# Taking whole turns off in PSUM: the phases of the kernel generation move from VectorE to TensorE

## The chip, the cores and the metric

One core of a Trainium2 chip runs the program. The time is the device time of one execution in microseconds; the kernel before was timed three times and its median is given. A profile of one further execution shows what each engine did.

## The reference

Four layers are applied to a sequence of 2048 rows of 640 channels: a state-space convolution, attention, the same convolution and the same attention again, each on the layer-normed input and added to it. The part that matters here is the kernel `K` of the convolution, which both convolution layers use:

```python
dt = jnp.exp(log_dt)[:, None]
A = A_re + 1j * A_im
logdA = dt * A
dB = dt * Bc
P = jnp.exp(logdA[:, :, None] * l[None, None, :])
K = jnp.einsum("dn,dnl,dn->dl", Cc, P, dB).real
...
y = irfft2(rfft2(u padded) * rfft2(K padded))[..., :L] + u * Dskip
```

For each of 640 channels and 2048 positions, `K` is a sum over 128 states of a complex exponential. Its size is the exponential of a real number that grows with the position, and its angle is a phase that grows with it too, many whole turns in all.

## The kernel before, in words

The program first generates `K` (`kgen`), then transforms it, and then runs the layers. The generation splits the position in a coarse and a fine part, so that the exponential is a product of two factors, and sums over the states with matmuls. `kg_tables` computes, per channel and state, the numbers from which all sizes and angles follow, splits each in three bf16 parts and sends them through DRAM into three tables: `tb` (48 rows), `ta` and `tm` (96 rows). A matmul of a table's 48 or 96 rows with the constants in `kg` (0, 1, 2, ... in blocks) then makes 512 columns of angles or sizes at once.

The loop in `_kgen` has 20 units of 32 channels, `u` from 0 to 19, and works on several at once. In iteration `u`, for unit `u`, `u + 1`, `u - 1` and so on:

- `sizes(u, k)`, k = 0, 1, 2: two matmuls each of 512 columns into the PSUM tile `pe` (L404, two buffers), and `exps(u, k)`, an exponential of it on ScalarE (L412, L414).
- `phase_first(u + 1, h)`, h = 0, 1: two matmuls of 512 columns into the PSUM tile `ph` (L371, one buffer), from `tb` (48 rows) for h = 0 and from `ta` (96 rows) for h = 1. The result is an angle in turns.
- `phase(u + 1, h)`: VectorE rounds it to whole turns by adding and subtracting `MAGIC`, 1.5 x 2^23 (L191, into the tile `r`), and subtracts the whole turns (L381, into `f`, four buffers).
- `trig(u, h)`: ScalarE takes the absolute value of `f` (L394), the sine of `f` (L395) and the cosine by way of the absolute value (L396).
- `products(u - 1, k)`: six VectorE operations of 1024 columns that multiply sizes by sines and cosines (L422 to L431).
- `sums(u - 2, ds)`: eight groups of 16 small matmuls (L441) that sum over the states into the PSUM tile `pk`.
- `store(u - 3)`: ScalarE copies `pk` out (L450), and every fourth unit goes to DRAM.

In eight iterations, and after the loop's end, `stats` adds two statistics operations and their merge on VectorE. The order of the instructions on TensorE, ScalarE and VectorE is the order in which the loop writes them (`manual_schedule`), with even and odd iterations written differently so that ScalarE's exponentials and sines need one change of its table per iteration. After the last `sizes` the tables' memory is freed (`early.close()`) and the weights of the first transform are loaded into it.

Of the kernel before, what the change touches and what calls it, by code (L numbers as in the profile page):

```python
# [11 lines left out]
F32 = mybir.dt.float32  # L12
F32R = mybir.dt.float32r
BF16 = mybir.dt.bfloat16
I32 = mybir.dt.int32
AF = mybir.ActivationFunctionType
ALU = mybir.AluOpType
# [4 lines left out]
P = 128  # L22
# [5 lines left out]
MAGIC = 1.5 * 2.0**23  # L28
TWO_PI = 2.0 * math.pi
# [25 lines left out]
def host_constants():  # L55
    i = np.arange(64)
    jh = np.arange(2)
    base = (32 * i[None, :] + 16 * jh[:, None]).reshape(P)
    t = np.arange(8)
    j = np.arange(2)  # L60
    l = base[:, None, None] + t[None, :, None] + 8 * j[None, None, :]
    k1 = np.arange(256)
    ang = (l[..., None] * (4 * k1 + 1)) % 8192
    th = 2.0 * np.pi * ang / 8192.0
    cs = np.stack([np.cos(th), -np.sin(th)], axis=-2)
    cs = cs.reshape(P, 8, 2, 2, 2, P)
    wf = np.ascontiguousarray(cs).astype(np.float32)
    wi = np.ascontiguousarray(cs.transpose(5, 1, 2, 3, 4, 0) / 2048.0).astype(np.float32)

    col = np.arange(32)  # L70
    r1 = np.zeros((96, 16, 32), np.float32)
    r2 = np.zeros((96, 16, 32), np.float32)
    r3 = np.zeros((96, 16, 64), np.float32)
    r4 = np.zeros((96, 16, 32), np.float32)
    for d in range(16):
        for part in range(3):
            row = 16 * part + d
            r1[row, d] = col + 1
            r2[row, d] = col
            r2[48 + row, d] = 1  # L80
            r3[row, d] = 32 * np.arange(64)
            r4[row, d] = col
            r4[48 + row, d] = 1
    kg = np.concatenate([r.reshape(96, -1) for r in (r1, r2, r3, r4)], axis=1)

    ob = np.zeros((P, 6, 64), np.float32)
    for r in range(D):
        ob[r % P, r // P, r // 20] = 1
    ob[32:52, 5, 32] = 1

    row = np.zeros((66, L), np.float32)
    row[0:64:2] = 1
    row[64:] = -1
    return {
        "c_ob": ob.reshape(P, -1),
        "c_row": row,
        "c_wf": wf.reshape(P, -1),
        "c_wi": wi.reshape(P, -1),
        "c_kg": kg.astype(ml_dtypes.bfloat16),
        "c_id": np.eye(P, dtype=np.float32),  # L100
    }
# [55 lines left out]
class Net:  # L157
# [152 lines left out]
    def _kgen(self, ctx):  # L310
        tc, nc, ins = self.tc, self.nc, self.ins
# [5 lines left out]
        ta = sp.tile([96, 8, 5, P], BF16, name="ta")  # L317
        tb = sp.tile([48, 8, 5, P], BF16, name="tb")
        tm = sp.tile([96, 8, 5, P], BF16, name="tm")
        kg = sp.tile([96, 2560], BF16, name="kg")  # L320

        with tc.tile_pool(name="kgq", bufs=1) as pp:
            SH = [P, 5, NST]
# [23 lines left out]

        units = [(q, r, q * 256 + 16 * r, 128, 128) for q in range(2) for r in range(8)]
        units += [(2, r, 512 + 16 * r, 64, 64) for r in range(4)]
        C1, S1, C2, S2, M1, M2, E1R, F, PH, PE_, PK, KST = ({} for _ in range(12))  # L350
        KST[0, 0] = bp.tile([P, 64, 32], F32, tag="kst", bufs=2, name="kst00")

        def big(tag, u, x, bufs=2):
# [8 lines left out]
        def grp(table, u, par, rows):  # L362
            d = units[u][2] + par * units[u][3]
            return table[0:rows, d % 128 // 16, d // 128]

        def phase_first(u, h):

            pp = PH[u, h] = kp.tile([P, 1024], F32, tag="ph", bufs=1, name=f"ph{u}{h}")
            src, col, rows = ((tb, 0, 48), (ta, 512, 96))[h]
            for par in range(2):  # L370
                nc.tensor.matmul(pp[:, 512 * par : 512 * par + 512], grp(src, u, par, rows),  # L371
                                 kg[0:rows, col : col + 512], start=True, stop=True)

        def phase(u, h):
            if (u, h) not in PH:
                phase_first(u, h)
            pp = PH.pop((u, h))
            r = bp.tile([P, 1024], BF16, tag="r", bufs=2, name=f"r{u}{h}")
            self.magic_round(r, pp)
            F[u, h] = bp.tile([P, 1024], F32, tag="f", bufs=4, name=f"f{u}{h}")  # L380
            nc.vector.tensor_tensor(F[u, h], pp, r, ALU.subtract)  # L381

        def trig(u, h):
            if h == 0:
                C1[u], S1[u] = big("c1", u, 33), big("s1", u, 33)
                nc.gpsimd.memset(C1[u][:, :, :, 0:1], 1.0)
                nc.gpsimd.memset(S1[u][:, :, :, 0:1], 0.0)
                s, c = swap(S1[u])[:, :, :, 1:33], swap(C1[u])[:, :, :, 1:33]
            else:
                C2[u], S2[u] = big("c2", u, 32, 3), big("s2", u, 32, 3)  # L390
                s, c = swap(S2[u]), swap(C2[u])
            f = F.pop((u, h))
            fa = bp.tile([P, 1024], F32, tag="fa", bufs=1, name=f"fa{u}{h}")
            nc.scalar.activation(fa, f, AF.Abs)  # L394
            nc.scalar.activation(s, f.rearrange("p (a d s) -> p a d s", a=2, d=16), AF.Sin, scale=TWO_PI)  # L395
            nc.scalar.activation(c, fa.rearrange("p (a d s) -> p a d s", a=2, d=16), AF.Sin,  # L396
                                 scale=-TWO_PI, bias=self.halfpi)

# [17 lines left out]
        def products(u, k):  # L416

            tt = nc.vector.tensor_tensor
            if k == 0:
                E1R[u] = big("e1r", u, 64, 2)  # L420
                er, m1, c1 = (fl(a[u]) for a in (E1R, M1, C1))
                tt(er[:, :, 32:64], m1[:, :, 32:64], c1[:, :, 0:32], ALU.mult)  # L422
                tt(er[:, :, 0:32], m1[:, :, 0:32], c1[:, :, 32:0:-1], ALU.mult)
            elif k == 1:
                m1, s1 = (fl(a.pop(u)) for a in (dict(M1), S1))
                nc.vector.scalar_tensor_tensor(m1[:, :, 32:64], m1[:, :, 32:64], -1.0, s1[:, :, 0:32],
                                               op0=ALU.mult, op1=ALU.mult)
                tt(m1[:, :, 0:32], m1[:, :, 0:32], s1[:, :, 32:0:-1], ALU.mult)
            else:
                tt(C2[u], C2[u], M2[u], ALU.mult)  # L430
                tt(S2[u], S2[u], M2[u], ALU.mult)  # L431
# [34 lines left out]
        with tc.manual_schedule(engines=engines):  # L466
            for h in range(2):
                phase(0, h)
            for u in range(n + 3):
                now, nxt, prod, tot = u < n, u + 1 < n, 0 < u <= n, 2 <= u < n + 2  # L470
                odd = u % 2 == 1
                if u >= 3:
                    store(u - 3)
                if now and not odd:
                    trig(u, 0)
                if prod:
                    products(u - 1, 0)
                if now:
                    sizes(u, 0)
                    if odd:  # L480
                        exps(u, 0)
                if nxt:
                    phase_first(u + 1, 0)
                if tot:
                    sums(u - 2, range(0, 2))
                if now:
                    sizes(u, 1)
                    if odd:
                        exps(u, 1)
                if tot:  # L490
                    sums(u - 2, range(2, 3))
                if nxt:
                    phase(u + 1, 0)
                if now and odd:
                    sizes(u, 2)
                    exps(u, 2)
                if prod:
                    products(u - 1, 1)
                if now:
                    trig(u, 0 if odd else 1)  # L500
                if tot:
                    sums(u - 2, range(3, 5))
                if nxt:
                    phase(u + 1, 1)
                if prod:
                    products(u - 1, 2)
                if tot:
                    sums(u - 2, range(5, 7))
                if now:
                    if odd:  # L510
                        trig(u, 1)
                    else:
                        exps(u, 0)
                        sizes(u, 2)
                        exps(u, 1)
                        exps(u, 2)
                if tot:
                    sums(u - 2, range(7, 8))
                if u == 0:
                    self.load_x()  # L520
                    nc.sync.dma_start(self.ident, ins["c_id"])
                if 5 <= u < 13:
                    self.stats(u - 5)
                for t in {n: range(8, 12), n + 1: range(12, 16)}.get(u, ()):
                    self.stats(t)
                if u == n:
                    early.close()
                    self.conv_weights(nc.gpsimd)
# [831 lines left out]
```

## Time and profile before

| | |
|---|---|
| median of three runs | 3025.67 us (3024.11 to 3025.82) |
| the profiled execution | 3025.52 us, its span 3023.7 us |
| TensorE busy | 2797.2 us (93%), 21696 matmuls |
| ScalarE busy | 2427.3 us (80%) |
| VectorE busy | 1402.3 us (46%) |
| mean granted clock of TensorE | 0.958 |
| the generation's loop | from about 53 us to 300 us |

The whole span is dominated by the attention layers, where ScalarE and TensorE are nearly full; the shares of the whole span say nothing about the generation, which is one twelfth of it. Every number for the change has to be read from that stage. [...]

### The profile page before, as it was taken

How to read it: one execution, taken by the hardware profiler on the slowest of the kernel's cores; microseconds unless marked ns; L12 is line 12 of the kernel's file. 1: busy time of each engine (PE TensorE's matmuls, PEld its weight loads, DVE VectorE, ACT ScalarE, POOL GpSimd, SP SyncE). 2: the span in 40 equal slices, each digit the busy share in tenths (PEclk: the TensorE clock that was granted, in tenths of full speed). 3: DMA queues.
4: the chain of work that ended last, by engine and by line, in shares of the span. 5: the costliest groups of instructions: out<-in, count | busy, mean ns of one | idle time of the engine just before them, and what ended most of it. 6: DMA issues, size and time to landing. Idle time of an engine off the chain costs nothing. (4 is left out here: it accounts for less than half of the span.)

```text
span 3023.7 us, 52365 instructions
## 1 busy us (share of the span) xinstructions
PE 2797.2 (93%) x21696; PEld 1284.0 (42%) x21696; DVE 1402.3 (46%) x1788; ACT 2427.3 (80%) x2910; POOL 45.1 (1%) x117
## 2 busy tenths in 40 slices
PE   2776989998999999999999899798999999999998
PEld 0333979775233323333232689673233333323333
DVE  7999899942123232322323499721222223222222
ACT  5888333444999999999999532438999999999997
POOL 0001000000000000000000000000000000000000
PEclk9855999999999999999999999899999999999999
DMA  6114531133200010000100211131100101110100
GB/s 145 33 22 112 186 143 56 46 115 111 80 22 25 22 27 21 26 25 22 25 22 20 113 56 42 58 131 56 27 24 23 43 22 26 39 28 21 43 19 23
DMA packets 109104, 158.82 MB, mean 53 GB/s; under 512 B 58948, under 2 KB 65092, under 8 KB 105236
## 3 DMA queue, kind: packets, MB, share of 16 engines
q1 hardware_dynamic: 102680, 137.70, 15.7%
q0 software_dynamic: 4208, 16.67, 1.5%
q8 instruction: 175, 2.87, 0.4%
q10 hardware_dynamic: 1968, 0.98, 0.1%
q14 instruction: 73, 0.60, 0.1%
HBM read 95.22 MB, written 48.04 MB: 47 GB/s over the span
## 5 line engine op out<-in xcount | busy, mean ns | idle before, releaser
L1158 ACT ACTIVATE pt<-scb 128x1024 f32<-128x1024 f32 x1024 | 942.2, 1116 | 7.5 <-DMA qpb<-mxd 4.5
L1158 ACT ACTIVATE pt<-scd 128x1024 f32<-128x1024 f32 x1024 | 942.2, 1117 | 7.0 <-PE scd L1154 5.4
L1168 PE MATMUL pod<-pt,vt 128*32 128x512 f32 x4096 | 547.1, 606 | 4.4 <-DVE on L1185 0.2
L1168 PE MATMUL pob<-pt,vt 128*32 128x512 f32 x4096 | 547.0, 606 | 4.4 <-DVE on L1185 0.3
L1154 PE MATMUL scb<-qpb,kt 62*128 62x512 f32 x2048 | 385.9, 451 | 6.2 <-DVEq L1103 5.8
L1154 PE MATMUL scd<-qpd,kt 62*128 62x512 f32 x2048 | 385.9, 451 | 5.6 <-PEq L1103 5.3
L1154 PEld LDWEIGHTS scb<-qpb,kt 62*128 62x128 f32 x2048 | 165.9, 185 | 402.1 <-ACT pt L1158 392.6
L1154 PEld LDWEIGHTS scd<-qpd,kt 62*128 62x128 f32 x2048 | 166.0, 185 | 401.7 <-ACT pt L1158 392.4
L1216 DVE TENSOR_TENSOR x<-pyd,x 128x320 f32<-128x320 f32 x146 | 71.8, 492 | 560.8 <-PE pyd L1228 560.8
L1216 DVE TENSOR_TENSOR x<-pyb,x 128x320 f32<-128x320 f32 x146 | 71.8, 492 | 547.6 <-PE pyb L1228 547.6
L1188 DVE RECIPROCAL rc<-rc 128x512 f32<-128x512 f32 x62 | 207.9, 3354 | 2.1
L1168 PEld LDWEIGHTS pob<-pt,vt 128*32 128x32 f32 x4096 | 80.6, 108 | 178.2 <-issue 160.2
L1168 PEld LDWEIGHTS pod<-pt,vt 128*32 128x32 f32 x4096 | 80.6, 108 | 178.0 <-issue 160.0
L601 PE MATMUL za<-xna,wf 128*128 128x256 f32 x512 | 113.0, 383 | 2.5 <-ACT xna L757 2.5
L601 PE MATMUL zc<-xnc,wf 128*128 128x256 f32 x512 | 111.5, 379 | 2.7 <-ACT xnc L757 2.7
L603 ACT ACTIVATE Aa<-za 128x1024 f32<-128x1024 f32 x16 | 16.4, 1023 | 118.5 <-PE za L601 117.3
L603 ACT ACTIVATE Ac<-zc 128x1024 f32<-128x1024 f32 x16 | 16.4, 1023 | 113.7 <-PE zc L601 113.7
L1228 PE MATMUL pyd<-wo,ot 128*32 128x320 f32 x1168 | 105.3, 432 | 0.0
L1228 PE MATMUL pyb<-wo,ot 128*32 128x320 f32 x1168 | 105.3, 432 | 0.0
L601 PEld LDWEIGHTS za<-xna,wf 128*128 128x128 f32 x512 | 97.8, 192 | 16.6 <-ACT xna L757 3.3
L601 PEld LDWEIGHTS zc<-xnc,wf 128*128 128x128 f32 x512 | 96.9, 190 | 16.3 <-ACT xnc L757 3.3
L800 PE MATMUL yc<-Ac,wi 128*128 128x128 f32 x640 | 78.4, 286 | 15.8 <-DVE Ac L114 13.1
(312 smaller groups left out, 3107.2 us busy)
## 6 DMA issues: line engine op xcount, KB each, us to landing
kh<-kh SPq DMA_DIRECT2D x10, 2048.0 KB
kh<-kn SPq DMA_DIRECT2D x5, 2048.0 KB
qhd<-qh SPq DMA_DIRECT2D x40, 256.0 KB
qld<-ql SPq DMA_DIRECT2D x40, 256.0 KB
qpb<-qhd SPq DMA_DIRECT2D x256, 40.0 KB
qpd<-qhd SPq DMA_DIRECT2D x256, 40.0 KB
ot<-on SPq DMA_DIRECT2D x216, 40.0 KB
wf<-in_c_wf POOLq DMA_DIRECT2D x16, 512.0 KB, 7.9
```

The costliest lines, as they stand in the source:

```text
L601: nc.tensor.matmul(zv[:, :, c, kk], self.wf[:, t + 4 * h, j, c, kk], x, start=(n == 0), stop=(n == 3))
L603: nc.scalar.activation(A.rearrange("p (o s) d -> p o s d", o=2)[:, :, 2 * t : 2 * t + 2], z.rearrange("p (c o e) -> p o c e", c=2, o=2), A ...
L800: nc.tensor.matmul(y[:, s * DC : (s + 1) * DC], self.wi[:, t, j, c_, kk], v[:, 2 * t + c_, kk], start=(i == 0 and not whole), stop=(i == 3 ...
L1154: nc.tensor.matmul(sc[:, 512 * par : 512 * par + 512], kt[rows, 128 * t : 128 * t + 128], qps[nb, hg, pr][rows], start=True, stop=True)
L1158: nc.scalar.activation(pt, sc, AF.Exp, scale=SCALE)
L1168: nc.tensor.matmul(po[32 * j : 32 * j + 32], vt[:, t], pts[step, j // 2][:, 512 * (j % 2) : 512 * (j % 2) + 512], start=(t == 0), stop=(t ...
L1188: nc.vector.reciprocal(rc, rc)
L1216: nc.vector.tensor_tensor(xh, py, xh, ALU.add)
L1228: nc.tensor.matmul(py[j : j + m], o[:, 128 * i + j : 128 * i + j + m], w[:, 320 * half : 320 * half + 320], start=start, stop=stop)
```

## The change

The rounding constant now enters in PSUM. For each half of a phase tile, TensorE accumulates four matmuls in the same place: the angle, a matmul of one row that adds `MAGIC`, one of one row that adds `-MAGIC`, and the angle again with negated constants. What is left is the whole turns minus the angle, so the sine gets the opposite scale. VectorE's `phase` is one copy of 1024 columns out of PSUM. The absolute values for h = 1 are made by a new `fold` on VectorE, which clears the sign bit; those for h = 0 stay on ScalarE. `phase_first(u + 1, 1)` stands earlier on TensorE's queue: before the sums 3 and 4 of iteration `u`, where it was behind them. `kg` gets the negated blocks (3584 columns where it had 2560), and GpSimd fills the three constants of `unit` once.

```diff
-    kg = np.concatenate([r.reshape(96, -1) for r in (r1, r2, r3, r4)], axis=1)
+    kg = np.concatenate([r.reshape(96, -1) for r in (r1, r2, r3, r4, -r1, -r2)], axis=1)
...
-        kg = sp.tile([96, 2560], BF16, name="kg")
+        kg = sp.tile([96, 3584], BF16, name="kg")
+        unit = sp.tile([1, P + 2], BF16, name="unit")
+        nc.gpsimd.memset(unit[:, 0:P], 1.0)
+        nc.gpsimd.memset(unit[:, P : P + 1], MAGIC)
+        nc.gpsimd.memset(unit[:, P + 1 : P + 2], -MAGIC)
...
         def phase_first(u, h):
-            pp = PH[u, h] = kp.tile([P, 1024], F32, tag="ph", bufs=1, name=f"ph{u}{h}")
+            ph = PH[u, h] = kp.tile([P, 1024], F32, tag="ph", bufs=1, name=f"ph{u}{h}")
             src, col, rows = ((tb, 0, 48), (ta, 512, 96))[h]
             for par in range(2):
-                nc.tensor.matmul(pp[:, 512 * par : 512 * par + 512], grp(src, u, par, rows),
-                                 kg[0:rows, col : col + 512], start=True, stop=True)
+                o, w = ph[:, 512 * par : 512 * par + 512], grp(src, u, par, rows)
+                nc.tensor.matmul(o, w, kg[0:rows, col : col + 512], start=True, stop=False)
+                for k in range(2):
+                    nc.tensor.matmul(o, unit[:, 0:P], unit[:, P + k : P + k + 1].to_broadcast([1, 512]),
+                                     start=False, stop=False)
+                nc.tensor.matmul(o, w, kg[0:rows, 2560 + col : 3072 + col], start=False, stop=True)
 
         def phase(u, h):
...
-            pp = PH.pop((u, h))
-            r = bp.tile([P, 1024], BF16, tag="r", bufs=2, name=f"r{u}{h}")
-            self.magic_round(r, pp)
+            ph = PH.pop((u, h))
             F[u, h] = bp.tile([P, 1024], F32, tag="f", bufs=4, name=f"f{u}{h}")
-            nc.vector.tensor_tensor(F[u, h], pp, r, ALU.subtract)
+            nc.vector.tensor_copy(F[u, h], ph)
+
+        def fold(u):
+            FA[u] = bp.tile([P, 1024], F32, tag="fb", bufs=1, name=f"fb{u}")
+            nc.vector.tensor_scalar(FA[u].bitcast(I32), F[u, 1].bitcast(I32), 0x7FFFFFFF, None,
+                                    ALU.bitwise_and)
...
-            fa = bp.tile([P, 1024], F32, tag="fa", bufs=1, name=f"fa{u}{h}")
-            nc.scalar.activation(fa, f, AF.Abs)
-            nc.scalar.activation(s, f.rearrange("p (a d s) -> p a d s", a=2, d=16), AF.Sin, scale=TWO_PI)
+            if h == 0:
+                fa = bp.tile([P, 1024], F32, tag="fa", bufs=1, name=f"fa{u}{h}")
+                nc.scalar.activation(fa, f, AF.Abs)
+            else:
+                fa = FA.pop(u)
+            nc.scalar.activation(s, f.rearrange("p (a d s) -> p a d s", a=2, d=16), AF.Sin, scale=-TWO_PI)
...
                 if prod:
                     products(u - 1, 0)
+                if now and not odd:
+                    fold(u)
...
                 if prod:
                     products(u - 1, 1)
+                if now and odd:
+                    fold(u)
+                if nxt:
+                    phase_first(u + 1, 1)
                 if now:
                     trig(u, 0 if odd else 1)
```

More of the change, by code (lines that the diff above doesn't have):

```diff
@@ L349, in _kgen @@
         units += [(2, r, 512 + 16 * r, 64, 64) for r in range(4)]
-        C1, S1, C2, S2, M1, M2, E1R, F, PH, PE_, PK, KST = ({} for _ in range(12))
+        C1, S1, C2, S2, M1, M2, E1R, F, FA, PH, PE_, PK, KST = ({} for _ in range(13))
         KST[0, 0] = bp.tile([P, 64, 32], F32, tag="kst", bufs=2, name="kst00")
```

## The prediction

> **What bounds the kernel now.** The change lies in the generation of the convolution kernels, the loop over `u` at the start of the program. I read first which engine is full there (busy time by stretch), then what each instruction group costs (groups of instructions), then the exact spacing on VectorE and TensorE (instructions in order of time), and last the granted clock.
>
> ```profile
> core 0: us, PE busy (x) PEld busy (x) DVE busy (x) ACT busy (x) POOL busy (x), PEclk, DMA share, GB/s
> 192.00:204.00 12.00, 7.38 (x120) 3.53 (x120) 11.93 (x13) 11.94 (x13) 0.31 (x2) 0.50 0.01 1
> 204.00:216.00 12.00, 10.00 (x155) 4.54 (x154) 11.83 (x14) 8.47 (x10) 0.94 (x2) 0.50 0.01 1
> ```
>
> VectorE works 23.76 of these 24 us, ScalarE 20.41, TensorE 17.38 with a granted clock of one half. VectorE bounds the loop, and its groups and spacing are these:
>
> ```profile
> L381 DVE TENSOR_TENSOR f<-ph,r 128x1024 f32<-128x1024 f32 x40 | 49.0, 1225 | 2.0
> L191 DVE TENSOR_SCALAR r<-ph 128x1024 bf16<-128x1024 f32 x40 | 48.7, 1218 | 8.2 <-PE ph L371 7.9 <-DMA hdare<-hare 0.3
> L394 ACT ACTIVATE fa<-f 128x1024 f32<-128x1024 f32 x40 | 42.1, 1052 | 6.0 <-DVE f L381 5.3
> ...
> 269.18 1.22 DVE L191 TENSOR_SCALAR r<-ph 128x1024 bf16<-128x1024 f32 x1
> 270.43 1.22 DVE L381 TENSOR_TENSOR f<-ph,r 128x1024 f32<-128x1024 f32 x1
> 271.57 1.22 DVE L426 SCALAR_TENSOR_TENSOR m<-m,s 128x1024 f32<-128x1024 f32 x1
> 272.70 1.22 DVE L428 TENSOR_TENSOR m<-m,s 128x1024 f32<-128x1024 f32 x1
> ```
>
> Start to start, a rounding takes 1.25 us, a subtraction 1.14, a product 1.13. One iteration has two roundings, two subtractions and six products: 2 x 2.39 + 6 x 1.13 = 11.6 us, and in some iterations the statistics of `x` besides. The pace of the whole loop comes from the first matmul of `sizes` in iteration 2 and in iteration 19:
>
> ```profile
> 73.56 1.03 PE L404 MATMUL pe<-kg,tm 48*128 48x512 bf16 x2
> ...
> 278.98 1.03 PE L404 MATMUL pe<-kg,tm 48*128 48x512 bf16 x2
> ```
>
> That is 205.4 us for 17 iterations, 12.08 us each. The iterations before and after hold few or no phase matmuls beside sums, and what follows (the spectra of the kernels) starts from the loop's end, so I carry a gain or loss of the 17 iterations to the end of the program one for one.
>
> **What VectorE and ScalarE gain.** Of each phase the rounding goes and the subtraction becomes a copy out of PSUM. No copy of 1024 columns is in the trace. The rows near it are the rounding, which reads the same PSUM tile (1218 ns), and this one of half the width:
>
> ```profile
> L1185 DVE COPY on<-pob 128x512 f32<-128x512 f32 x31 | 21.4, 692 | 133.3 <-PE pob L1168 117.2 <-DMA qpb<-qhd 16.1
> L278 DVE TENSOR_SCALAR ph<-th 128x640 f32<-128x640 f32 x1 | 0.5, 486 | 0.0
> ```
>
> Between 692 ns and twice that lies 1.2 us; I take 1.14 start to start. The fold of one half's absolute values onto VectorE is one operation per iteration on SBUF: 486 ns for 640 columns in the second row would make some 0.65 us for 1024, and the rounding's 1.22 us is the upper end. An iteration on VectorE so falls by 2 x 1.25 and rises by 0.65 (up to 1.2): it gains 1.85 us (1.3 at worst) and ends at 10.2 us of 12.08. ScalarE loses one absolute value of 1.05 us per iteration: its share of the 24 us above is 85%, 10.3 us of 12.08, which becomes 9.2. Were nothing else changed, the loop would gain 17 x 1.85 = 31 us.
>
> **What TensorE gets.** For each half of each phase tile one matmul becomes four: the angle, two of one row with the constants, and the negated angle again. That is 12 more matmuls of 512 columns per iteration. Their price, and what TensorE does already, is read where it runs without waiting, in iteration 6 and into 7:
>
> ```profile
> 131.37 1.03 PE L404 MATMUL pe<-kg,tm 48*128 48x512 bf16 x2
> 132.19 1.06 PE L371 MATMUL ph<-kg,tb 48*128 48x512 bf16 x2
> 133.18 0.44 PE L441 MATMUL pk<-e1r,c 128*32 128x64 f32 x8
> 133.39 0.44 PE L441 MATMUL pk<-m,s 128*32 128x64 f32 x8
> ...
> 134.19 1.03 PE L404 MATMUL pe<-kg,tm 48*128 48x512 bf16 x2
> 135.16 0.44 PE L441 MATMUL pk<-e1r,c 128*32 128x64 f32 x8
> 135.37 0.44 PE L441 MATMUL pk<-m,s 128*32 128x64 f32 x8
> 135.74 1.03 PE L404 MATMUL pe<-kg,tm 96*128 96x512 bf16 x2
> 136.71 0.44 PE L441 MATMUL pk<-e1r,c 128*32 128x64 f32 x8
> ...
> 137.72 1.03 PE L371 MATMUL ph<-kg,ta 96*128 96x512 bf16 x2
> 138.69 0.44 PE L441 MATMUL pk<-e1r,c 128*32 128x64 f32 x8
> ...
> 139.75 0.44 PE L441 MATMUL pk<-m,s 128*32 128x64 f32 x8
> 140.13 0.60 PE L404 MATMUL pe<-kg,tm 48*128 48x512 bf16 x2
> ```
>
> Two matmuls of 512 columns last 1.03 us together and, at the doubled clock of the last row, 0.60: the second starts 0.43 us after the first at half clock and half of that later at full clock. Eight small ones of `sums` take 0.21 us (133.18 to 133.39), so the 128 of an iteration 3.4 us. From 131.37 to 140.13 lies one whole iteration's work without a wait: 8.76 us, made of 10 matmuls of 0.427 us, eight pairs of 0.427 us and some 1.1 us of small gaps where the kinds change. Twelve more matmuls are 5.1 us at half clock: **13.8 us per iteration, more than the 12.08 of now and far more than VectorE's 10.2**. At full clock the whole is about 7 us, and VectorE stays the bound. So everything hangs on the clock that is granted.
>
> **The clock.** The granted clock changes on a grid of 3.41 us. Two of its climbs:
>
> ```profile
> 133.31:136.72 3.41, 3.41 (x55) 1.40 (x54) 3.38 (x4) 1.17 (x2) 0.16 (x1) 0.50 0.02 1
> 136.72:140.13 3.41, 3.41 (x84) 2.23 (x83) 3.41 (x4) 3.29 (x4) 0.14 (x1) 0.50 0.02 5
> 140.13:143.55 3.42, 1.30 (x15) 0.32 (x12) 3.39 (x4) 3.39 (x4) 0.02 (x1) 1.00 0.00 0
> ...
> 232.30:235.70 3.40, 3.40 (x56) 1.39 (x52) 3.37 (x4) 1.07 (x3) 0.16 (x1) 0.50 0.07 13
> 235.70:239.10 3.40, 3.21 (x82) 2.13 (x82) 3.40 (x4) 3.37 (x4) 0.00 (x0) 0.50 0.00 0
> 239.10:242.50 3.40, 1.33 (x16) 0.22 (x4) 3.37 (x3) 3.37 (x4) 0.16 (x1) 1.00 0.00 0
> ```
>
> The first window of each group is as busy as can be, and the clock stays at one half after it; the second is no busier, and after it the clock is full for one window, in which TensorE has little left to do, and then falls. What sets the second window apart is its kind of work: 80 of the small matmuls on 128 rows and one pair on 96 rows, against some 50 small ones and pairs on 96 and on 48 rows. If I weigh each matmul's time by its rows out of 128, with the starts above, 133.31 to 136.72 comes to 1.28 + 0.85 x 0.375 + 0.85 x 0.75 = 2.24 us of 3.41 (0.66), and 136.72 to 140.13 to 2.2 + 0.64 = 2.84 (0.83). I therefore read the gate as one that looks at rows in use, with a climb at about three quarters. The falls are after windows as empty as 1.30 of 3.41; from them I estimate that a full clock is lost below about a third.
>
> The added matmuls have 48, 96 and one row. By this reading the 3.4 us of a phase weigh 0.19 (half 0) or 0.375 (half 1) and never lift the clock by themselves. Only the stretches of `sums` can: in even iterations four groups, the pair of `sizes` on 96 rows and a fifth group, 3.26 us long and worth 1.71 + 0.64 + 0.43 = 2.78 (0.81 when a window falls on it exactly, still above 0.72 when it is up to 0.5 us late or 0.95 early); in odd ones five groups in a row, with about 0.95 us of tolerance. The chance of a climb is 1.45 of 3.41 and 0.95 of 3.41, about 0.35 per iteration. Because 27.6 us, two iterations, are close to eight windows, hits come in series with long pauses, so I take a little less, six climbs in 17 iterations. After one the next window holds a matmul pair of `sizes`, the phase of half 0 and three groups, some 1.2 of 3.41: right at the point where the clock falls again. One full window saves up to 3.4 us; if it holds, the run goes on until TensorE must wait for VectorE's copies, some 6.5 us saved after an even iteration and 2 after an odd one. Six climbs at 3.3 us on average are 20 us.
>
> **The sum.** 17 x (13.8 - 12.08) = 29 us lost at half clock, 20 us won back by climbs, 1 us won before iteration 2, where two VectorE operations fewer lie on the way: 8 us in all. The profiled execution took 3025.5 us, as the median of 3025.7 does within 0.2 us; the forecast is **3034 us**. Covered costs: the third more of `kg` to load (0.2 MB) sits behind tables that VectorE needs until 43 us, the three small memsets of GpSimd lie before the first matmul; uncovered, a microsecond. `phase_first` of half 1 now stands ahead of sums on TensorE's queue and waits for the copy of half 0: at half clock three groups and a `sizes` pair (2.4 us) lie between, more than the copy's 1.2, so the sums behind it do not wait.
>
> **Rivals.** *The clock counts any busy time.* Then a TensorE that never idles runs at full clock, at 7 us per iteration, VectorE bounds at 10.2, and 17 x 1.85 = 31 us are won, less some 2 for waits on ScalarE: **2996 us**. For it: nothing here shows a one-row matmul, and weights other than rows fit the climbs too. Against it: the window of 133.31. It decides where the clock holds through the phases. [...]
>
> *The clock never climbs* (one-row matmuls count as idle, or grid and loop miss each other): TensorE at 13.8 us per iteration, 28 us lost, **3053 us**. For it: the climbs need a fit within a microsecond. Against it: the old loop does climb, as the two groups above show.
>
> *The change does little*: climbs come often enough that 13.8 falls to 12.1, 3026 us, the point of no change: eight or nine climbs, or longer ones. It is the lower part of the forecast's own range, 3018 to 3048.
>
> **How the numbers follow.** Forecast's case 0.55 (of it slower 0.36, same 0.11, faster 0.08), counts-anything 0.28 (faster 0.26, same 0.02), never-climbs 0.12 (slower), something else 0.05, spread. The three middle outcomes use 0.2%, 6 us, which is about what can be told from no change. Faster 0.36, same 0.15, slower 0.49. The range 2996 to 3053 reaches from the middle of the fast rival to that of the slow one and leaves out about half of each.
>
> **What would show it.** Right: TensorE busy near 12.00 of 12.00 in stretches between 75 and 290 us, VectorE and ScalarE below 85%, VectorE's copy waiting for the phase matmul, granted clock mostly 0.50 with single windows of 1.00, the pair of `sizes` of iteration 19 some 8 us later. Wrong: a granted clock near 1.00 from iteration 2 on with VectorE full at 10.2 us per iteration; or copies and folds far off 1.2 and 0.65 us; or a loss that lies outside the loop. Because the grid need not start with the program, I expect its times to scatter more from run to run than the 1.7 us of before.

## The result and the profile after

The changed kernel takes 3055.36 us (median of four runs, 3054.66 to 3058.29) against 3024.89 us before (3023.11 to 3025.82): a ratio of 1.0104, interval 1.0091 to 1.0116. It is slower by 30 us; the forecast was 3034 and the range ended at 3053.

The head of the changed kernel's page, then busy time by stretch, in the columns of the prediction's table (PE is TensorE, PEld its weight loads, DVE VectorE, ACT ScalarE and POOL GpSimd, each with its count, then the granted clock, DMA share and GB/s):

```profile
span 3056.5 us, 52775 instructions
PE 2897.5 (95%) x21936; PEld 1302.3 (43%) x21936; DVE 1367.1 (45%) x1768; ACT 2406.0 (79%) x2890; POOL 52.9 (2%) x120
...
192.00:204.00 12.00, 12.00 (x104) 3.55 (x100) 7.96 (x10) 5.14 (x6) 0.31 (x2) 0.50 0.40 52
204.00:216.00 12.00, 12.00 (x149) 4.81 (x149) 8.41 (x10) 9.20 (x10) 0.58 (x1) 0.58 0.01 1
```

TensorE is busy in all 24 us. VectorE, 23.76 of 24 us before, has 16.37; ScalarE has 14.34 instead of 20.41. The bound has moved to TensorE. The groups of instructions between 50 and 335 us (busy us, mean ns, then idle time before them) and the waits between 72 and 310 us (in total, times, longest) say the same:

```profile
L381 PE MATMUL ph<-unit 1*128 1x512 bf16 x152 | 71.4, 566 | 0.0
L391 DVE COPY f<-ph 128x1024 f32<-128x1024 f32 x38 | 46.4, 1222 | 70.9 <-PE ph L383 70.9
L396 DVE TENSOR_SCALAR fb<-f 128x1024 int32<-128x1024 int32 x20 | 13.7, 686 | 0.0
...
DVE f L391 <- PE ph L383: 58.0, 25, 3.3
ACT m L431 <- PE pe L423: 33.3, 8, 4.8
ACT m L433 <- PE pe L423: 28.9, 11, 4.3
```

VectorE stands idle before its copy (L391) until the last angle matmul (L383) is done, and ScalarE stands idle before its exponentials until `sizes` (L423) are. The copy costs 1222 ns, as the rounding did, and the fold 686 ns.

The instructions of TensorE in order of time (start, duration) give the pace. It is read from start to start, as the durations overlap: in the changed kernel the angle matmul at 191.97 us lasts 0.61 us and the next one starts 0.54 us after it. Shown are the first matmul of `sizes` of iteration 2 in the kernel before, then those of iterations 2 and 19 in the changed kernel; that of iteration 19 before is the prediction's row at 278.98 us.

```profile
66.87 1.03 PE L404 MATMUL pe<-kg,tm 48*128 48x512 bf16 x2
```

```profile
73.87 1.03 PE L423 MATMUL pe<-kg,tm 48*128 48x512 bf16 x2
...
308.55 1.03 PE L423 MATMUL pe<-kg,tm 48*128 48x512 bf16 x2
```

The first place moved by 7.0 us, the second by 29.57 (308.55 against 278.98). So 7.0 us are lost before iteration 2 and 22.6 between the two places, where 12.48 us per iteration became 13.80. (The row at 73.56 us in the prediction is the second pair of `sizes` of iteration 2 and not the first.) The last of the sums ends 29.56 us later, too. The profiled execution loses some 3 us more behind the loop, most of it between 620 and 750 us, where the program is unchanged; the medians differ by 30.5, so little of that belongs to the change.

### The profile page after: what moved, and what is told of

It reads as the page before. It is cut to its first block, busy times and chain, and to the rows that moved or that the text cites. A ratio compares the mean times of both kernels' runs of the same rounds, so it can differ in the third digit from the quotient of the medians.

```text
span 3056.5 us, 52775 instructions
## 1 busy us (share of the span) xinstructions
PE 2897.5 (95%) x21936; PEld 1302.3 (43%) x21936; DVE 1367.1 (45%) x1768; ACT 2406.0 (79%) x2890; POOL 52.9 (2%) x120
## 3 DMA queue, kind: packets, MB, share of 16 engines
q8 instruction: 178, 2.92, 0.4%
## 5 line engine op out<-in xcount | busy, mean ns | idle before, releaser
L628 ACT ACTIVATE Ac<-zc 128x1024 f32<-128x1024 f32 x16 | 16.4, 1024 | 114.0 <-PE zc L626 112.9
```

The costliest lines, as they stand in the source:

```text
L628: nc.scalar.activation(A.rearrange("p (o s) d -> p o s d", o=2)[:, :, 2 * t : 2 * t + 2], z.rearrange("p (c o e) -> p o c e", c=2, o=2), A ...
```

## The experiments

Three theories stood against each other for a loss of 30 us where 8 were forecast. **Rows**: the few rows of the added matmuls keep the clock low, and each change of the row count costs time besides. **Data or busy time**: the clock follows something else. **Other engines**: the fold or the early phase of half 1 delays the chain. Each group of runs was taken beside runs of the kernel before (3024.1 to 3025.0 us).

**rows_zero** and **rows_ones** give the constant matmuls 128 rows. In the first, one row of the weights holds ones and 127 hold zeros, and the constant stands in every row of the other operand; in the second, all weights are ones and the constant is divided by 128:

```diff
-        unit = sp.tile([1, P + 2], BF16, name="unit")
+        unit = sp.tile([P, P + 2], BF16, name="unit")
...
-  nc.tensor.matmul(o, unit[:, 0:P], unit[:, P + k : P + k + 1].to_broadcast([1, 512]), ...)
+  nc.tensor.matmul(o, unit[:, 0:P], unit[:, P + k : P + k + 1].to_broadcast([P, 512]), ...)
   # rows_zero: unit[1:128, 0:P] = 0;  rows_ones: all ones, constants MAGIC / 128
```

> The two constant matmuls of a phase half get 128 rows instead of one (row 0 carries the constant, 127 rows of weights are zero); the sums are the same. Theory, the gate weighs matmul time by rows in use: a phase then weighs 0.69 (half 0) or 0.88 (half 1) instead of 0.19 and 0.38, nearly every window of 3.41 us lies above the climb at 0.7 and all lie above the fall at a third, so the granted clock is near 1.00 through the loop, TensorE takes some 7.5 us per iteration, VectorE bounds at 10.2, and the time is about 3000 us (2994 to 3008). Rival, the gate looks at data that toggle: rows of zeros count nothing, the clock stays at one half, 3055 us. Rival, the gate looks at busy time and the added matmuls cost by their columns alone: 3055 us as well.

> As the run with 128 rows, but all 128 rows carry a weight of one and the constant divided by 128, so that no operand is zero. Theory of rows: the same as with rows of zeros, about 3000 us, clock near 1.00 in the loop. Rival of toggling data: faster here only, 3000 us against 3055 with zeros. Rival of busy time: 3055 us.

Measured: rows_zero 3010.74 us (ratio 0.9956, interval 0.9939 to 0.9973), rows_ones 3002.96 (0.9934, 0.9918 to 0.9951). The same matmuls, in the same order and number, are 45 to 52 us faster on 128 rows than on one. Rows of zero weights do most of it: an iteration takes 10.97 us in rows_zero and 11.06 in rows_ones, and of the 5.5 us between their profiled executions 4.0 lie before iteration 2. So it isn't the values of the weights. The time of rows_zero lies 3 us above the range that was expected of it, as its iterations take 10.97 us and not VectorE's 10.2. In rows_ones the first matmul of `sizes` stands at 68.92 us in iteration 2 and at 256.91 in iteration 19: 11.06 us per iteration where the changed kernel has 13.80. Its busy time by stretch, and its waits (72 to 260 us):

```profile
204.00:216.00 12.00, 8.86 (x154) 3.87 (x154) 12.00 (x12) 11.97 (x14) 1.50 (x3) 1.00 0.58 74
...
PE ph L379 <- DVE f L391: 29.8, 18, 3.5
DVE f L391 <- PE ph L383: 9.9, 9, 1.4
```

In these 12 us the clock is full, VectorE and ScalarE are full, and over the whole stretch the wait has turned round: TensorE waits for the copy three times as long as the copy for TensorE. The mean granted clock from 72 to 260 us is 0.88.

**no_const** leaves the two constant matmuls out, so that the phases are zero:

```diff
-                for k in range(2):
-                    nc.tensor.matmul(o, unit[:, 0:P], unit[:, P + k : P + k + 1].to_broadcast([1, 512]), ...)
```

> Leaves out the two constant matmuls, so that angle and negated angle cancel and every phase is zero; all else stays. Theory, TensorE at half clock is the bound: 8 matmuls of 0.43 us less and the gaps beside them, about 4.4 us of 14.6 per iteration at half clock, which leaves 10.2 to 10.6 us, level with VectorE's 10.2; the time is 3025 - 17 x 1.6 = 2998 us (2993 to 3006). Rival, the loss comes from the earlier place of half 1 on TensorE's queue or from VectorE: a gain of less than 10 us, 3045 us or more.

Measured: 3004.81 us (0.9938, 0.9921 to 0.9954), within the expected range. Leaving 80 matmuls of each constant out is no better than giving them 128 rows: an iteration takes 11.31 us, against 11.06 in rows_ones. The granted clock from 72 to 260 us is 0.69 here and 0.88 in rows_ones, so the likely reason is that on 128 rows they pay for themselves by the clock that they keep up; no run separated the two.

**rows_same** gives the constant matmuls as many rows as the angle matmuls around them (48 or 96), with weights of zero but for row 0. Nothing then changes the row count within a phase:

```diff
-  unit[:, 0:P], unit[:, P + k : P + k + 1].to_broadcast([1, 512])
+  unit[0:rows, 0:P], unit[0:rows, P + k : P + k + 1].to_broadcast([rows, 512])
```

> The two constant matmuls of a group get as many rows as its angle matmuls (48 in half 0, 96 in half 1), with zeros in all rows of the constant but row 0; their number, order and results stay. Theory (a change of the number of rows costs 0.10 to 0.15 us, and few rows keep the clock down): the pairs at L381 and L383 of the changed kernel take 0.43 and 0.86 us at half clock instead of 0.54 and 0.96; a window that lies in half 1 weighs about 0.7 or more and lifts the clock, one in half 0 about 0.4 and just keeps it; 10.0 to 12.5 us per iteration, 3005 to 3030 us. Rival A (the time goes with the constant operand or with the accumulation of three matmuls into one place, not with the rows): the gaps stay at 0.54 and 0.96, and the time is 3040 or more unless the clock rises. Rival B (only 128 rows lift the clock): 13.6 us per iteration, 3050.

Measured: 3004.64 us (0.9930, 0.9913 to 0.9947), 11.12 us per iteration, at the fast end of what was expected. A phase of half 1 at half clock, first in the changed kernel, then in rows_same:

```profile
191.97 0.61 PE L379 MATMUL ph<-kg,ta 96*128 96x512 bf16 x1
192.51 1.03 PE L381 MATMUL ph<-unit 1*128 1x512 bf16 x2
193.47 0.61 PE L383 MATMUL ph<-kg,ta 96*128 96x512 bf16 x1
193.87 0.63 PE L379 MATMUL ph<-kg,ta 96*128 96x512 bf16 x1
194.43 1.03 PE L381 MATMUL ph<-unit 1*128 1x512 bf16 x2
195.40 0.61 PE L383 MATMUL ph<-kg,ta 96*128 96x512 bf16 x1
195.93 0.34 PE L460 MATMUL pk<-e1r,c 128*32 128x64 f32 x4
```

```profile
79.91 0.59 PE L380 MATMUL ph<-kg,ta 96*128 96x512 bf16 x1
80.29 1.06 PE L382 MATMUL ph<-unit 96*128 96x512 bf16 x2
81.14 0.63 PE L385 MATMUL ph<-kg,ta 96*128 96x512 bf16 x1
81.57 0.63 PE L380 MATMUL ph<-kg,ta 96*128 96x512 bf16 x1
82.00 1.06 PE L382 MATMUL ph<-unit 96*128 96x512 bf16 x2
82.85 0.63 PE L385 MATMUL ph<-kg,ta 96*128 96x512 bf16 x1
83.41 0.44 PE L462 MATMUL pk<-e1r,c 128*32 128x64 f32 x8
```

From 96 rows to one the next matmul starts after 0.54 to 0.56 us instead of 0.38 to 0.43, and from the pair of one row back to 96 after 0.96 instead of 0.85. A phase takes 3.96 us (191.97 to 195.93) instead of 3.50 (79.91 to 83.41). Two phases per iteration make 0.92 us. The rival, that the constant operand or the accumulation of several matmuls costs the time, has fallen: both are the same in rows_same.

**abs_scalar** undoes the fold, so ScalarE again takes both absolute values:

```diff
-            if h == 0:
-                fa = ...; nc.scalar.activation(fa, f, AF.Abs)
-            else:
-                fa = FA.pop(u)
+            fa = ...; nc.scalar.activation(fa, f, AF.Abs)
...
-                    fold(u)
```

> The absolute values of half 1 go back to ScalarE; no fold on VectorE. Theory, neither VectorE nor ScalarE bounds the changed loop: 3055 us, within 4. Rival, VectorE is still on the path: up to 17 x 0.65 = 11 us faster, 3044. Rival, ScalarE is: up to 17 x 1.05 = 18 us slower, 3073.

Measured: 3054.57 us (1.0104, 1.0087 to 1.0121), as the changed kernel. Here, where TensorE sets the pace, half of the absolute values can stand on either engine.

**late_half1** takes back the earlier place of half 1 on TensorE's queue:

```diff
-                if nxt:
-                    phase_first(u + 1, 1)
```

> The changed kernel with the phases of half 1 issued where the kernel before issues them, behind the abs of half 0; constant matmuls, copy and fold stay. Theory (TensorE's own matmuls set the pace of the iteration): the order in which the same matmuls are issued changes nothing, 3055 plus or minus 5 us, 13.8 us per iteration between the first matmuls of sizes of iterations 2 and 19. Rival (the early place makes the sums and products of an iteration wait behind the phases, and that is part of the loss): 3030 to 3045. Rival on the other side (the early place is what keeps VectorE from waiting): 3065 or more.

Measured: 3061.12 us (1.0121, 1.0104 to 1.0137), 6 us beyond the changed kernel and just outside what was expected. The profiled execution is the slowest of the four, 3066.85 us. Two consecutive first matmuls of `sizes` in its loop, and its busy time from 72 to 260 us:

```profile
148.26 1.03 PE L423 MATMUL pe<-kg,tm 48*128 48x512 bf16 x2
...
163.02 1.03 PE L423 MATMUL pe<-kg,tm 48*128 48x512 bf16 x2
...
72.00:260.00 188.00, 187.65 (x1898) 62.88 (x1896) 135.97 (x142) 130.23 (x133) 10.76 (x27) 1.00 0.17 27
```

An iteration at half clock is 14.76 us, and fourteen of the 17 between iterations 2 and 19 are just that, eleven of them in a row. Only two are short, 11.96 and 12.29 us, between 252 and 276 us. (The clock column says 1.00 here, but a pair lasts 1.03 us as at half clock in all runs. The column has no entry before the first change and then shows 1.00; durations decide.) The order matters after all, but not by a wait: TensorE is busy for 187.65 of 188 us. Between iterations 2 and 19 the clock of this execution climbed once, for two windows, and that of the changed kernel eight times. Which matmuls fall together into one window of the clock depends on their order; that this makes the whole 6 us of the medians is not shown.

**rows_96** starts from rows_ones and lets the remaining matmuls of 48 rows use 96, with zeros in the added ones:

```diff
-        tb = sp.tile([48, 8, 5, P], BF16, name="tb")
+        tb = sp.tile([96, 8, 5, P], BF16, name="tb")
+        nc.gpsimd.memset(tb, 0.0)
...
-            src, col, rows = ((tb, 0, 48), (ta, 512, 96))[h]
+            src, col, rows = ((tb, 0, 96), (ta, 512, 96))[h]
...
-                par, col, rows = (k, 1024 + 512 * h, 48) if k < 2 else (h, 2048, 96)
+                par, col, rows = (k, 1024 + 512 * h, 96) if k < 2 else (h, 2048, 96)
```

> The kernel with constants of 128 rows of MAGIC/128 (rows_ones), and besides 96 rows instead of 48 in the angle matmuls of half 0 and in the sizes of k below 2; the added rows are zeros. Theory (the gate weighs rows, and what is left of the half clock in rows_ones comes from its matmuls of 48 rows): nearly every window of the generation weighs over 0.7, the clock stays full, 9.5 to 10.0 us per iteration, where rows_ones has 11.06; 17 iterations by 1.1 to 1.5 us less: 2978 to 2986 us against 3003. Rival (rows_ones is already held by VectorE or ScalarE, or by the idle time of TensorE, and its cold windows come from that): 3000 to 3006.

Measured: 2998.60 us (0.9918, 0.9902 to 0.9935), the fastest of all and 26 us below the kernel before. But it takes 11.04 us per iteration, as rows_ones does: the theory missed by 12 us or more, and the rival was right about the pace, though its 3000 us was 1.4 too high. What is gained over rows_ones lies before iteration 2 (66.37 us against 68.92) and behind the loop. Two more runs asked what holds these 11 us, and what the padding is worth without the change.

**rows_96_abs** is rows_96 with the edit of abs_scalar. **before_96** is the kernel before with the edit of rows_96 and nothing of the change.

> rows_96 with the fold undone: the absolute value of half 1 is again an instruction on ScalarE (1.05 us), and VectorE has 0.69 us less per iteration. Theory (with TensorE's clock mostly full VectorE's 10.44 us of work per iteration, two copies, one fold and six products, hold the pace): up to 17 x 0.69 = 11.7 us less, less what ScalarE's longer work takes back: 2986 to 2994 us, against 2998.6 for rows_96. Rival A (the windows at half clock after TensorE has run ahead hold the pace): no change, 2996 to 3001. Rival B (ScalarE, whose work grows by 1.05 us per iteration, becomes the bound): slower, 3003 or more.

> The kernel before with 96 rows instead of 48 in the angle matmuls of half 0 and in the sizes of k below 2 (the added rows are zeros); nothing of the change is in it. Theory (the kernel before is held by VectorE's 12.2 us per iteration, two roundings, two subtractions and six products, and only now and then by TensorE's clock): 12.48 becomes 12.2, 17 x 0.28 = 5 us less, 3015 to 3022 us against 3024. Rival (most of what rows_96 gained comes from the padding alone and not from the change): 3000 to 3008. Rival on the other side (TensorE is not late there at all): 3023 to 3026.

Measured: rows_96_abs 3029.35 us (1.0016, 1.0006 to 1.0026), before_96 3024.13 (0.9997, 0.9987 to 1.0007). Busy time from 72 to 260 us of rows_96, rows_96_abs and before_96, in this order, a fence each, with three waits of rows_96_abs (the same stretch):

```profile
72.00:260.00 188.00, 146.09 (x2607) 72.76 (x2640) 176.50 (x180) 168.43 (x175) 16.04 (x40) 0.88 0.24 36
```

```profile
72.00:260.00 188.00, 139.19 (x2196) 67.40 (x2196) 147.39 (x145) 163.65 (x167) 6.40 (x32) 0.79 0.19 30
...
PE pe L421 <- ACT m L429: 28.2, 8, 5.4
ACT m L429 <- PE pe L421: 21.5, 7, 3.9
DVE e1r L439 <- PE pk L458: 19.8, 8, 4.3
```

```profile
72.00:260.00 188.00, 131.01 (x2137) 60.09 (x2138) 186.11 (x180) 165.14 (x169) 6.56 (x33) 0.61 0.17 26
```

In before_96 VectorE is busy for 186.11 of 188 us: it holds the pace, and a quicker TensorE changes nothing. I had expected 5 us; the run says none, as the second rival had it. In rows_96 VectorE is at 94%, ScalarE at 90%. Giving ScalarE back its 1.05 us per iteration costs some 30 us in all, and an iteration then takes 12.71 us. The rows show how: `sizes` waits for ScalarE's exponential to free its tile, ScalarE then waits for `sizes`, and VectorE waits for the sums behind them on TensorE's queue. So the fold, worth nothing at half clock, is what the gain rests on once the rows keep the clock up. Rival B of that run named ScalarE; the loss is larger than its own 17 x 1.05 = 18 us, and the waits that the three engines pass round are the likely rest, which no run separated.

## Why the prediction was wrong in size and right in kind

**The bound, as foreseen.** TensorE at 12.00 of 12.00, VectorE and ScalarE below 85%, the copy waiting for the phase: all as forecast. The copy at 1222 ns and the fold at 686 were within the forecast's bounds (0.65 from start to start was the estimate), and abs_scalar shows that neither counted.

**The step that failed first: 13.8 us per iteration at half clock.** Where no climb falls into it, an iteration of the changed kernel takes 14.76 us (even ones, for instance from 184.59 to 199.35 us) or 14.49 (odd ones). The sum took 0.427 us for each added matmul, from pairs of equal matmuls, and missed what a change between one row and 48 or 96 costs: 0.11 to 0.16 us, four times per phase, eight times per iteration. rows_same shows it: 0.92 us per iteration. Iteration 2 takes half a microsecond more, so 17 iterations at half clock come to 249.3 us: 15 us more than 17 x 13.8.

**The second: six climbs at 3.3 us.** Between iterations 2 and 19 the clock climbed eight times, more often than forecast, but 249.3 - 234.7 = 14.6 us is all that they saved, 1.8 each. No climb lasted more than its one window, where the forecast left it open whether the next one keeps the clock, and averaged. And after the climbs in even iterations TensorE, now ahead, waits for VectorE's copy of half 0 before it can start half 1, as `ph` has one buffer. Three of these waits, in brackets:

```profile
137.22 0.58 PE L379 MATMUL ph<-kg,ta 96*128 96x512 bf16 x1 [1.53 <-DVE f L391]
...
165.46 0.59 PE L379 MATMUL ph<-kg,ta 96*128 96x512 bf16 x1 [1.67 <-DVE f L391]
...
220.23 0.59 PE L379 MATMUL ph<-kg,ta 96*128 96x512 bf16 x1 [1.67 <-DVE f L391]
```

The six climbs in even iterations were each followed by such a wait of 0.5 to 1.7 us and saved 1.0 to 2.0 us; the two in odd ones met none and saved 2.7 each. The forecast worked out that the sums do not wait at half clock, and let TensorE wait for copies only where the clock holds for longer. Now windows on the clock's grid in the changed kernel, a climb and then no climb:

```profile
128.80:132.20 3.40, 3.40 (x83) 2.13 (x75) 3.40 (x4) 3.40 (x5) 0.00 (x0) 0.50 0.00 0
132.20:135.60 3.40, 3.40 (x58) 1.29 (x57) 3.37 (x6) 3.40 (x5) 0.02 (x1) 1.00 0.40 45
135.60:139.00 3.40, 1.87 (x12) 0.36 (x5) 3.40 (x4) 3.37 (x5) 0.53 (x1) 0.51 0.82 110
...
203.90:207.30 3.40, 3.40 (x53) 1.66 (x53) 3.02 (x3) 1.03 (x1) 0.00 (x0) 0.50 0.00 0
207.30:210.70 3.40, 3.40 (x9) 0.38 (x6) 1.07 (x2) 2.88 (x3) 0.58 (x1) 0.50 0.02 5
```

After the window with 83 matmuls, mostly sums on 128 rows, the clock is at 1.00; after the equally busy ones with 53 and 9 it stays at 0.50. At full clock TensorE is still busy for all 3.40 us of the next window, yet that window, with its phase of 48 rows and one, doesn't keep the clock: it falls at 135.6. If any busy time counted, as the first rival had it, this TensorE would have run at full clock throughout; the window from 203.90, busy for 3.40 us and followed by another at 0.50, does not agree, and in rows_zero, with rows of zero weights in the same matmuls, the clock does rise (its mean from 72 to 260 us is 0.92, against 0.64 in the changed kernel).

**The third: 1 us won before iteration 2.** Seven were lost. Iterations 0 and 1 hold all their phase matmuls and no sums, and the forecast put the added ones there at nothing. The two iterations, first in the kernel before, then in the changed one (the clock column has no entry yet):

```profile
53.05:59.38 6.33, 4.52 (x11) 1.11 (x11) 3.20 (x3) 3.73 (x4) 0.00 (x0) 1.00 0.14 32
59.38:66.87 7.49, 4.82 (x12) 0.81 (x11) 7.42 (x8) 5.75 (x6) 0.15 (x1) 1.00 0.14 32
```

```profile
52.41:63.38 10.97, 10.51 (x22) 1.67 (x23) 1.97 (x2) 3.01 (x3) 0.00 (x0) 1.00 0.14 32
63.38:73.87 10.49, 10.49 (x23) 1.70 (x22) 6.84 (x7) 6.67 (x7) 0.73 (x2) 1.00 0.14 31
```

TensorE, which idled for a third of them, is now busy for 21.0 of 21.5 us. They grew by 7.6 us, and the loop begins 0.6 us earlier (so the larger `kg`, two fifths more and not a third, costs nothing that shows).

**A place misread.** The row at 73.56 us, taken for the first matmul of `sizes` of iteration 2 before, is the second pair of that iteration; the first stands at 66.87, ahead of VectorE. By equal places the kernel before ran 212.1 / 17 = 12.48 us per iteration, not 12.08, and the sum counted 7 us too much between the places and 8 too little ahead of them. That the two nearly cancel is chance.

**The sum again.** By equal places 249.3 - 212.1 = 37.2 us are lost at half clock, less 14.6 for the climbs, plus 7.0 before iteration 2: 29.6 us, as measured. The forecast had 29, 20 and -1. Against its 8 us the half clock makes 8 more (15, about what the row changes cost, less 7 for the misread pace), the climbs 5, the start 8.

**The rivals.** The rival of any busy time, at 0.28, fell with rows_zero: the rows make the difference. Its 2996 us is nearly what rows_96 reaches, but not by its sum: an iteration takes 11.04 us there and not 10.2. The rival of little change counted on eight or nine climbs; eight came, at 1.8 us each. The rival that never climbs named 3053 us, close to the result by luck: the clock did climb, and what the row changes took covered what the climbs gave. That times would scatter more from run to run is seen weakly, 3.6 us against 2.7.

## What to carry to other kernels

At half clock a pair of these matmuls lasted 1.03 us on one row and 1.03 to 1.06 on 128, but the pairs of one row did less to lift the clock (its mean from 72 to 260 us is 0.64 on one row and 0.92 in rows_zero): where a step moves to TensorE, look at its rows, and try padding them with zeros if the stage runs at half clock. Price an added matmul in its own surroundings and not from a run of equal ones: here each change of the row count added 0.11 to 0.16 us to the 0.43. And a gain on an engine off the path, like the fold, showed here only when the bound in front of it was gone (nothing in abs_scalar, some 30 us in rows_96_abs): test the parts in the state in which they are to be used.

## What the runs showed of the hardware

- **The clock rose with the rows.** rows_zero and rows_same change only the rows of the constant matmuls, and the mean granted clock from 72 to 260 us rises from 0.64 to 0.92 and 0.84. (In the changed kernel the column has no entry before 104.9 us and shows 1.00 there; from 108 to 252 us its mean is 0.56.) An estimate from the starts: weigh each matmul's time in a window of 3.41 us, the step in which the clock changes in the traces before and after (at half clock 0.427 us for 512 columns and 0.027 for a small one, at full clock half of that), by its rows out of 128. In the changed kernel's loop the eight windows that are followed by a full clock come to 0.67 to 0.77, and all others at half clock to 0.68 or less; in the kernel before, those followed by a full clock come to 0.71 to 0.81, and the others to 0.64 or less. So the 0.67 that climbed and the 0.68 that didn't leave the limit open: rows alone don't tell everything near it. In the two loops a full clock was lost after windows of 0.31 or less. Two windows of rows_same at about 0.35, each with the one behind it:

```profile
161.90:165.30 3.40, 2.92 (x56) 1.38 (x55) 3.37 (x6) 3.40 (x5) 0.00 (x0) 1.00 0.00 0
165.30:168.70 3.40, 0.15 (x1) 0.10 (x1) 3.40 (x5) 3.40 (x5) 0.55 (x1) 1.00 0.69 82
...
138.00:141.40 3.40, 2.94 (x43) 1.30 (x41) 3.37 (x6) 3.40 (x5) 0.00 (x0) 1.00 0.03 5
141.40:144.80 3.40, 0.99 (x18) 0.52 (x17) 3.40 (x5) 3.40 (x4) 0.55 (x1) 0.51 0.00 0
```

  Both first rows are equally busy (2.92 and 2.94 us) and weigh 0.35 by this estimate. The one with 48 small matmuls on 128 rows keeps the clock (1.00 behind it); the one with 32 and a whole phase on 48 rows loses it (0.51). The changed kernel's window from 132.20 us, shown above, is busy for all of its 3.40 us, weighs 0.31 and loses it: in these windows busy time didn't decide.
- **A change of the row count cost TensorE 0.11 to 0.16 us** at half clock between one row and 96 (0.54 to 0.56 and 0.96 us from start to start in the changed kernel, 0.38 to 0.43 and 0.85 in rows_same). Between 96 and 128 rows rows_zero shows none (0.40 and 0.86 us from start to start), between 48 and 128 it does (0.51 and 0.97).
- **GpSimd's memset of 128x32 took longer while the fold ran on VectorE.** In the changed kernel's loop the 18 that start during a fold take 0.55 to 0.58 us, the 18 others 0.15 to 0.16; in the kernel before, which has no fold, the means of its two lines are 155 and 157 ns. In abs_scalar, without the fold, GpSimd is busy for 5.91 us from 72 to 260 us (29 instructions), in the changed kernel for 11.73 (30). A fold, the memset that starts during it, and a later one:

```profile
79.66 0.69 DVE L396 TENSOR_SCALAR fb<-f 128x1024 int32<-128x1024 int32 x1
79.89 0.55 POOL L402 MEMSET c<- 128x32 f32 x1 [7.39 <-DVE e1r L442]
...
83.86 0.15 POOL L403 MEMSET s<- 128x32 f32 x1 [3.42 <-DVE m L447]
```

  None of the waits above is for it.
